# The query fold moved from the end of the tile loop to tile 5, with the raw weights as moving side

## The chip, the cores and the metric

The kernel runs on one core of a Trainium2 chip. A core has five engines, each with a queue of its own that it works through in order: TensorE (PE, matmuls; its weight loads are listed as PEld), VectorE (DVE), ScalarE (ACT), GpSimd (POOL) and SyncE (SP, which issues most of the DMA transfers). In this kernel PE reads SBUF and writes into eight PSUM banks of 128 x 512 floats, out of which ACT and DVE read. The metric is the device time of one launch in microseconds (us). Profiles come from one execution of the program under the hardware profiler.

## The reference

For 2048 tokens x of width 512 the reference computes two branches and mixes them with a gate per token.

```python
# branch A: linear attention, 32 heads of width 16
q, k, v = split(x @ wqkv)                       # [head, token, 16]
pq, pk  = q @ w_phi[head], k @ w_phi[head]      # a 16x16 matrix per head
phi(p)  = concat(softmax(p), softmax(-p))       # 32 features
kv = phi(pk)^T @ v ;  z = phi(pk)^T @ 1
a  = concat_heads(phi(pq) @ kv / (phi(pq) @ z + 1e-6)) @ wo
# branch B: product-key experts, 32 heads, top 1 of 16 x 16
s1, s2 = (x @ w_q)[..., :128] @ k1^T, (x @ w_q)[..., 128:] @ k2^T
e = 16 * argmax(s1) + argmax(s2)                # one of 256 experts per head
b = sum_heads gelu(x . u[e]) * v[e]             # the softmax over one candidate is 1
g = sigmoid(sum(x * gate_w)) ;  y = g * a + (1 - g) * b
```

Since w_phi acts on q right behind the projection, the kernel multiplies it into the weights: x @ (wq_A @ w_phi) gives pq in one product. This product of weights is called a fold; there is one for k and one for q. In the same way the keys k1 and k2 are multiplied into w_q, which gives score weights of 512 x 1024.

## The kernel before, in words

Tokens go in 16 tiles of 128 (NT = 16). Every matrix that feeds a large matmul is held as two parts, a rounded high part and the rest (xh and xl for the tokens, wah and wal, wbh and wbl, sh and sl, eh and el, uh and ul), and a product takes three matmuls per block of 128 (`proj` and `mm3`, lines 53 to 58 and 87). `split` (line 49) makes the two parts: ACT copies the high part, DVE subtracts.

The program has a fixed order per engine: the text of the kernel is the order of each queue. It has three stages.

Start (lines 251 to 295). PE does 16 matmuls on a zeroed tile, warm. v's weights come in (wbh, wbl), the first v tiles are projected, and k's weights are folded (`fold_k`): for each of 4 x 4 blocks the small matrix wp stands as 32 x 32 weights and 512 columns of the raw matrix move through, so that the output is the transposed fold. Four blocks of it are then turned on PE (`fold_turn`) and split into wah and wal.

Tile loop (line 304). Tile t loads x for tile t + 3, projects v (`vproj`) and k (`kproj`, whose four DVE operations take the softmax differences out of PSUM), takes exponentials on ACT (line 346), sums and reciprocals on DVE and a product on POOL (`ksoft`, lines 198 to 202), and every second tile sums phi(k)^T v into one bank (`kvacc`). Between these, the plan of line 302 spreads 16 steps that make the score weights: `score_w` multiplies a raw matrix wq with the keys into a bank of the tag tr, after every second one `score_planes` copies the bank as two planes of 16-bit halves into wpl (ACT), and SP turns the planes with one DMA transpose into wtp. One tile later `score_join` puts the halves together again (ACT, line 237), and splits them into sh (ACT, line 241) and sl (POOL, line 242). The raw matrices wq0 to wq15 share two buffers of 8 KB a partition, so each load waits for the matmuls on the matrix two before it. rawq, q's raw weights, is the last in this row.

PSUM has four banks of the tag mm and three of the tag tr, each handed out in turn.

In tile 15, while the last score block is joined, PE works through `fold_q` (line 140) in two halves, with the first scores of the query stage (`front_s`, line 246) behind each. fold_q holds the raw weights as PE's weights and moves 32 columns of wp, 128 times; the output is not transposed, and ACT and DVE split it straight from PSUM into wah and wal, which k no longer needs (lines 153 and 154). Then come tile 15's exponential and `ksoft`.

Query stage (from line 672). PE finishes the sums of phi(k) (`kvz`, lines 213 to 218, which needs the d of tiles 14 and 15 from POOL's line 202), projects the first q tile (`front_q`) and the first expert products (`front_p`), spreads z over all partitions (`z_final`) and goes into a loop of 15 turns with scores, masks, q, attention and output. For the first mask (`mid_mask`, line 537) `best` finds the maxima on DVE and SP turns the mask with a DMA transpose (et, line 482).

```python
    nc = bacc.Bacc("TRN2", target_bir_lowering=False, num_devices=1)
```

This line of the host part (892) sets up the program; the area of SBUF for descriptors that POOL would write has its default size of 16 KB a partition.

Of the kernel before, what the change touches and what calls it, by code (L numbers as in the profile page):

```python
# [9 lines left out]
F32 = mybir.dt.float32  # L10
F32R = mybir.dt.float32r
BF16 = mybir.dt.bfloat16
U16 = mybir.dt.uint16
# [3 lines left out]
ALU = mybir.AluOpType  # L17
# [3 lines left out]
P = 128  # L21
S = 2048
D = 512
NT = S // P
NK = D // P
# [10 lines left out]
def mix_kernel(ctx, tc, xT, wqT, wkT, wv, wphi, wo, wq, kk, ug, ev, cst, out):  # L36
    nc = tc.nc
    pe, dve, act, pool, sp = nc.tensor, nc.vector, nc.scalar, nc.gpsimd, nc.sync
# [4 lines left out]
    def mm_bank(name):  # L43
        return psum.tile([P, 512], F32, tag="mm", bufs=4, name=name)

    def tr_bank(name):
        return psum.tile([P, 512], F32, tag="tr", bufs=3, name=name)

    def split(hi, lo, src):
        act.copy(hi, src)  # L50
        dve.tensor_tensor(lo, src, hi, op=ALU.subtract)  # L51
# [8 lines left out]
    kvb = per.tile([P, 8, 32], F32, name="kvb")  # L60
# [10 lines left out]
    wah = per.tile([P, NK, D], F32R, name="wah")  # L71
    wal = per.tile([P, NK, D], F32R, name="wal")
# [38 lines left out]
    w1 = cb.enter_context(tc_pool("w1", "right"))  # L111
    wa_ = ca.enter_context(tc_pool("wl", "left"))
    home = lambda t: late if t % 4 > 1 else w1

    wp = w1.tile([P, NK, 32], F32, bufs=1, name="wp")
    warm = w1.tile([P, 384], BF16, bufs=1, name="warm")
    rawx = {}

    def stage(src, name, shape=None):
        t_ = wa_.tile(shape or [P, NK, D], F32, tag="st", bufs=2, name=name)  # L120
        if src is not None:
            sp.dma_start(t_, src)
        return t_

    def x_load(t):
        r = rawx[t] = wa_.tile([P, NK, P], F32, tag="xr", bufs=3, name=f"xr{t}")
        if t > 0:
            sp.dma_start(r, xT[t])
# [3 lines left out]
        (dve.tensor_copy if t < 3 else act.copy)(xh[:, t, ks], r[:, ks])  # L132
        dve.tensor_tensor(xl[:, t, ks], r[:, ks], xh[:, t, ks], op=ALU.subtract)

    fv = lambda a, q: a.rearrange("p k (b c) -> p (k b) c", c=P)[:, :, 32 * q:32 * q + 32]

    def four(name):
        return [tr_bank(f"{name}{q}") if q < 3 else mm_bank(f"{name}{q}") for q in range(4)]

    def fold_q(raw, wh, wl):  # L140
        o = four("foldq")
        for i in range(2):
            for k in (2 * i, 2 * i + 1):
                for b in range(NK):
                    for q in range(4):
                        r = slice(32 * q, 32 * q + 32)
                        c0 = (k * NK + b) * 32
                        pe.matmul(o[q][:, c0:c0 + 32], raw[r, b, k * P:(k + 1) * P], wp[r, b, :],
                                  start=True, stop=True, skip_group_check=True)
            yield  # L150
        for q in range(4):
            part = o[q].rearrange("p (g c) -> p g c", c=32)
            act.copy(fv(wh, q), part)
            dve.tensor_tensor(fv(wl, q), part, fv(wh, q), op=ALU.subtract)
        yield

    def fold_k(raw, tmp):
        o = four("foldk")
        for j in range(NK):
            for q in range(4):  # L160
                r = slice(32 * q, 32 * q + 32)
                pe.matmul(o[q][32 * j:32 * j + 32, :], wp[r, j, :], raw[r, j, :], start=True, stop=True,
                          skip_group_check=True)
        for q in range(4):
            (act.copy if q < 2 else dve.tensor_copy)(tmp[q], o[q])

# [53 lines left out]
    def score_w(i, raw):  # L220
        j, par = i // 2, i % 2
        if par == 0:
            wsP[j] = tr_bank(f"ws{j}")
        for c in range(4):
            pe.matmul(wsP[j][32 * c:32 * c + 32, :], kp[:, j // 4, par, :], raw[:, c, :],  # L225
                      start=(par == 0), stop=(par == 1))

    def score_planes(j):
        pl = wa_.tile([P, 2, D], U16, tag="wpl", bufs=1, name=f"wpl{j}")
        act.copy(pl, wsP.pop(j).bitcast(U16).rearrange("p (c j) -> p j c", j=2))  # L230
        tp = wa_.tile([P, 8, P], U16, tag="wtp", bufs=1, name=f"wtp{j}")
        sp.dma_start_transpose(tp, pl.rearrange("p j c -> p (j c)"))
        joins.append((j, tp))

    def score_join(j, tp):
        tj = wa_.tile([P, D], F32, tag="wtj", bufs=1, name=f"wtj{j}")
        act.copy(tj.bitcast(U16).rearrange("p (k n j) -> p j k n", j=2, n=P),
                 tp.rearrange("p (j k) n -> p j k n", j=2))
        js = slice(P * j, P * j + P)
        t3 = tj.rearrange("p (k e) -> p k e", k=NK)  # L240
        act.copy(sh[:, :, js], t3)
        pool.tensor_tensor(sl[:, :, js], t3, sh[:, :, js], op=ALU.subtract)
# [8 lines left out]
    pool.memset(warm, 0.0)  # L251
    tab = w1.tile([P, 1], F32, bufs=1, name="tab")
    pool.memset(tab, 0.0)
    x_load(0)
# [12 lines left out]
    x_load(2)  # L267
    wps = mm_bank("warm")
    for _ in range(16):
        pe.matmul(wps[:, :384], warm[:, 1:P + 1], warm, start=True, stop=True)  # L270
    for a in sa + sb:
        pool.memset(a, 0)
    pool.memset(kvb, 0.0)
    pool.memset(ones, 1.0)
    for k in (0, 2, 1, 3):
        if k == 0:
# [13 lines left out]
    v2 = vproj(2)  # L290
    fold_turn(tk, wah, wal)
    v2()
    raws = [stage(wq[0], "wq0")]
    raws.append(stage(wq[1], "wq1"))
    pool.tensor_copy(wm, cs[:, 128:160].rearrange("p (a b) -> p a b", b=F))

    def spare(src, name, shape):
        t_ = wa_.tile(shape, F32, tag="xr", bufs=3, name=name)
        sp.dma_start(t_, src)
        return t_  # L300

    plan = {0: 2, 2: 1, 3: 1, 4: 2, 6: 2, 8: 2, 10: 2, 12: 2, 13: 1, 14: 1}
    done = 0
    for t in range(NT):
        if t + 3 < NT:
            x_load(t + 3)
        if 2 < t < NT - 2:
            vproj(t)()
        kproj(t)
        old = [] if t == NT - 3 else list(joins)  # L310
        if old:
            joins.clear()
        for _ in range(plan.get(t, 0)):
            score_w(done, raws[done])
            done += 1
            if done + 1 < 16:
                raws.append(stage(wq[done + 1], f"wq{done + 1}"))
            elif done == 15:
                rawq = stage(wqT, "rawq")
            if done % 2 == 0:  # L320
                score_planes(done // 2 - 1)
        if t == 11:
            rawu = [spare(ug[:, 0:2], "rawu0", [P, 2, NU])]
        if t == 12:
            rawu.append(spare(ug[:, 2:4], "rawu1", [P, 2, NU]))
        if t == 13:
            rawe = [spare(ev[:, 0], "rawe0", [P, D])]
        if t % 2 == 0:
            for u in (t - 3, t - 2):
                if u >= 0:  # L330
                    kvacc(u)
        if 0 < t < NT - 2:
            x_split(t + 2)
        if t == NT - 2:
            score_join(*old.pop())
# [10 lines left out]
        act.activation(phis[t], phis[t], AF.Exp)  # L346
        if t == NT - 2:
            score_join(*joins.pop())
# [5 lines left out]
        for j, tp in old:  # L354
            score_join(j, tp)
    ca.close()
    w2 = ctx.enter_context(tc_pool("w2", "left"))
    zb = w2.tile([P, 1024], F32, name="zb", bufs=1)
# [339 lines left out]
    for a in range(NT - 1):  # L698
        n, b, z = a + 1, a - 1, a - 2
# [77 lines left out]
    a, b, z = NT - 1, NT - 2, NT - 3  # L777
# [50 lines left out]
    ch, cl, o = st8[b]["c"]  # L828
# [71 lines left out]
```

## Time and profile before

| what | value |
|---|---|
| time, median of 3 runs | 380.48 us (379.95 to 380.8) |
| span of the profiled execution, first to last instruction | 378.1 us |
| what lies around the span, against the median | 2.4 us (that execution's own run time is not listed apart) |
| granted clock of PE, mean | 1.000 |
| busy PE / DVE / ACT / POOL | 372.5 / 315.9 / 235.5 / 154.9 us |
| rawq: issue, landing | 108.9 us, 5.7 us later |
| transfers of wq (1 MB), median to landing | 6.0 us |
| transposes of wpl, median to landing | 7.3 us |

How to read the lines of a profile: a row of the timeline is start, duration, engine, line of the kernel, operation, output<-inputs, shapes (output<-input; for PE the shape of the weights stands in front) and count, and in brackets how long the engine had been idle before and what ended it. SPq is the DMA-issuing queue of SP. A row of the groups gives the busy time and the mean duration in ns behind the first bar, and the idle time before behind the second. fp32r is the rounded high-part type. DMA rows give the size in KB and the time from issue to landing.

### The profile page before, as it was taken

The page shows a single profiled execution, that of the slowest core. Times are in us where ns is not written, and L with a number is a line of the kernel's source. Part 1 is how long each engine was busy: PE and PEld are TensorE (multiplying, and loading weights), DVE is VectorE, ACT ScalarE, POOL GpSimd, SP SyncE. Part 2 cuts the span into 40 slices and gives each one's busy share as a digit, 9 for nine tenths or more (in the row PEclk, how much of TensorE's full clock was granted, in tenths as well). Part 3 has the DMA queues.
Part 4 walks back from the last instruction along what each step waited for, and adds up shares of the span by engine and source line. Part 5 has one row for each costly group of instructions (what it writes and reads, how often), then busy time and mean ns, then how long its engine had stood idle before and what let it go on. Part 6 is the DMA issues. An engine that isn't in the chain of part 4 may idle for free.

```text
span 378.1 us, 9073 instructions
## 1 busy us (share of the span) xinstructions
PE 372.5 (99%) x3613; PEld 294.3 (78%) x3613; DVE 315.9 (84%) x776; ACT 235.5 (62%) x420; POOL 154.9 (41%) x164
## 2 busy tenths in 40 slices
PE   8999999999999999999999999999999999999996
PEld 4766777777768888888878888888888888888775
DVE  4479866866868968879999999999999999999993
ACT  4436554644646345769668777696686686687741
POOL 1014435325325232946427335344454454364700
PEclk9999999999999999999999999999999999999999
DMA  7757878478592034242351452441532524523201
GB/s 272 307 187 259 258 218 237 157 222 237 188 305 84 3 85 83 73 83 76 80 99 49 105 84 57 85 100 32 121 62 65 127 56 72 126 52 77 64 34 57
DMA packets 72219, 46.69 MB, mean 123 GB/s; under 512 B 63600, under 2 KB 64496, under 8 KB 69872
## 3 DMA queue, kind: packets, MB, share of 16 engines
q1 hardware_dynamic: 71312, 45.24, 44.6%
q10 hardware_dynamic: 864, 0.87, 0.8%
q8 instruction: 28, 0.46, 0.5%
q14 instruction: 15, 0.12, 0.1%
HBM read 26.43 MB, written 4.19 MB: 81 GB/s over the span
## 4 chain that ended last, share of the span: by engine, by line
PE 97%; DMA 1%; ACT 0%; SPq 0%; DVE 0%; issue 0%; ACTq 0%; DVEq 0%
PE po L627 11%; PE s L56 8%; PE s L57 8%; PE s L58 8%; PE po L634 5%; PE pq L56 5%; PE pv L56 4%; PE pk L56 4%; PE ws L225 4%; PE pv L57 4%; PE pq L58 4%; PE pk L57 4%; PE pq L57 4%; PE pk L58 4%; PE pv L58 4%; PE oT L518 3%
## 5 line engine op out<-in xcount | busy, mean ns | idle before, releaser
L432 POOL TENSOR_TENSOR w<-d,zb 128x512 f32<-128x512 f32 x32 | 40.9, 1294 | 83.4 <-ACT d L426 81.1
L202 POOL TENSOR_TENSOR d<-d,st 128x1024 f32<-128x1024 f32 x16 | 31.0, 1935 | 74.4 <-DVE st L201 40.5
L56 PE MATMUL s<-sh,xh 128*128 128x512 f32 x128 | 51.0, 399 | 0.0
L57 PE MATMUL s<-sl,xh 128*128 128x512 f32 x128 | 49.9, 390 | 0.0
L58 PE MATMUL s<-sh,xl 128*128 128x512 f32 x128 | 49.8, 389 | 0.0
L426 ACT ACTIVATE d<-d 128x512 f32<-128x512 f32 x32 | 20.1, 632 | 38.0 <-DVE d L98 29.3
L467 POOL TENSOR_TENSOR d<-d,st 128x512 f32<-128x512 f32 x30 | 31.2, 1062 | 28.5 <-DVE st L461 25.6
L509 ACT COPY pt<-tp 128x1024 uint16<-128x1024 uint16 x28 | 36.4, 1369 | 1.0 <-PE kvacc L209 1.0
L346 ACT ACTIVATE d<-d 128x1024 f32<-128x1024 f32 x16 | 17.0, 1064 | 28.5 <-DVE d L100 28.5
L499 ACT COPY pl<-d 128x1024 uint16<-128x1024 uint16 x28 | 29.2, 1045 | 4.4 <-POOL d L467 4.4
L58 PEld LDWEIGHTS s<-sh,xl 128*128 128x128 f32 x128 | 24.0, 188 | 5.1
L56 PEld LDWEIGHTS s<-sh,xh 128*128 128x128 f32 x128 | 24.0, 188 | 4.7
L57 PEld LDWEIGHTS s<-sl,xh 128*128 128x128 f32 x128 | 24.1, 188 | 4.5
L56 PE MATMUL pq<-wah,xh 128*128 128x512 f32 x64 | 26.7, 418 | 0.0
L56 PE MATMUL pv<-wbh,xh 128*128 128x512 f32 x64 | 26.0, 407 | 0.0
L436 DVE TENSOR_REDUCE st<-d 128x32 f32<-128x512 f32 x32 | 21.7, 683 | 5.0 <-ACT d L426 3.5
L57 PE MATMUL pv<-wbl,xh 128*128 128x512 f32 x64 | 25.2, 394 | 0.3 <-DVE wbl L51 0.3
L200 DVE TENSOR_REDUCE st<-d 128x64 f32<-128x1024 f32 x16 | 19.5, 1218 | 7.0 <-ACT d L346 7.0
L56 PE MATMUL pk<-wah,xh 128*128 128x512 f32 x64 | 25.3, 396 | 0.0
L58 PE MATMUL pv<-wbh,xl 128*128 128x512 f32 x64 | 25.1, 392 | 0.0
L58 PE MATMUL pq<-wah,xl 128*128 128x512 f32 x64 | 25.1, 392 | 0.0
L57 PE MATMUL pk<-wal,xh 128*128 128x512 f32 x64 | 25.0, 391 | 0.0
(177 smaller groups left out, 1029.5 us busy)
## 6 DMA issues: line engine op xcount, KB each, us to landing
wq<-wq SPq DMA_DIRECT2D x16, 1024.0 KB, 6.0
xr<-xT SPq DMA_DIRECT2D x15, 256.0 KB, 6.0
y<-ot SPq DMA_DIRECT2D x15, 256.0 KB, 2.3
rawk<-wkT SPq DMA_DIRECT2D x1, 1024.0 KB, 6.1
rawq<-wqT SPq DMA_DIRECT2D x1, 1024.0 KB, 5.7
rawo<-wo SPq DMA_DIRECT2D x4, 256.0 KB, 3.8
rawu<-ug SPq DMA_DIRECT2D x2, 258.0 KB, 6.3
rawv<-wv ACTq DMA_DIRECT2D x2, 256.0 KB, 4.2
```

The costliest lines, as they stand in the source:

```text
L56: pe.matmul(o, ah, bh, start=(first and i == 0), stop=False)
L57: pe.matmul(o, ah, bl, start=False, stop=False)
L58: pe.matmul(o, al, bh, start=False, stop=(last and i == n - 1))
L200: dve.tensor_reduce(st[:, 64:128], g64(d), axis=AX.X, op=ALU.add)
L202: pool.tensor_tensor(g64(d), g64(d), b64(st[:, 128:192]), op=ALU.mult)
L426: act.activation(hs(d, i), hs(d, i), AF.Exp)
L432: pool.tensor_tensor(hs(e["w"], i), hs(e["ph"], i), hs(zb, i), op=ALU.mult)
L436: dve.tensor_reduce(pair(e["st"][:, 64:128])[:, :, i], hs(e["ph"], i), axis=AX.X, op=ALU.add)
L467: eng.tensor_tensor(g64(d)[:, gs_], g64(d)[:, gs_], r[:, gs_].unsqueeze(2).to_broadcast([P, 32, F]), op=ALU.mult)
L499: act.copy(pl, e["ph"][:, halves[i]].bitcast(U16).rearrange("p (c j) -> p j c", j=2))
L509: act.copy(p16[:, :, 4 * i:4 * i + 4, :], e["tp"][i].rearrange("p (j g) n -> p j g n", j=2))
L627: pe.matmul(po, a, b, start=(i == 0), stop=False)
```

## The change

- The q fold moves from tile 15 to tile 5 and takes the form of the k fold: wp as 32 x 32 weights, the raw weights as moving side. Both folds now call one function, `fold`.
- Its output is transposed and must be turned. This is done as for the score weights: a copy into two planes of 16-bit halves (ACT), a DMA transpose (SP), a join (ACT) into a new tile wqf. Two of the four blocks go out in tile 5, two in tile 7; each is joined at the end of the tile behind it. `score_planes` becomes `turn_planes`, which also takes the function for the join.
- In tile 15 wqf is split into wah and wal with four ordinary splits, ahead of the score matmuls.
- rawq is loaded in the place of wq6, and each later wq load goes out one step later, wq7 behind the fold.
- wpl has two buffers instead of one, wtp three instead of one; wqf is new (8 KB a partition). The tile warm is gone, its matmuls read kvb, which is zeroed first for that.
- The descriptor area of POOL has 2 KB instead of 16.

```diff
-    warm = w1.tile([P, 384], BF16, bufs=1, name="warm")
+    warm = kvb.rearrange("p g c -> p (g c)").bitcast(BF16)
...
-    def fold_q(raw, wh, wl):
-        o = four("foldq")
-        for i in range(2):
-            for k in (2 * i, 2 * i + 1):
-                for b in range(NK):
-                    for q in range(4):
-                        r = slice(32 * q, 32 * q + 32)
-                        c0 = (k * NK + b) * 32
-                        pe.matmul(o[q][:, c0:c0 + 32], raw[r, b, k * P:(k + 1) * P], wp[r, b, :],
-                                  start=True, stop=True, skip_group_check=True)
-            yield
-        for q in range(4):
-            part = o[q].rearrange("p (g c) -> p g c", c=32)
-            act.copy(fv(wh, q), part)
-            dve.tensor_tensor(fv(wl, q), part, fv(wh, q), op=ALU.subtract)
-        yield
-
-    def fold_k(raw, tmp):
-        o = four("foldk")
+    def fold(raw, name):
+        o = four(name)
         for j in range(NK):
             for q in range(4):
                 r = slice(32 * q, 32 * q + 32)
                 pe.matmul(o[q][32 * j:32 * j + 32, :], wp[r, j, :], raw[r, j, :], start=True, stop=True,
                           skip_group_check=True)
+        return o
+
+    def fold_k(raw, tmp):
+        o = fold(raw, "foldk")
...
-    def score_planes(j):
-        pl = wa_.tile([P, 2, D], U16, tag="wpl", bufs=1, name=f"wpl{j}")
-        act.copy(pl, wsP.pop(j).bitcast(U16).rearrange("p (c j) -> p j c", j=2))
-        tp = wa_.tile([P, 8, P], U16, tag="wtp", bufs=1, name=f"wtp{j}")
+    def turn_planes(j, o, then):
+        pl = wa_.tile([P, 2, D], U16, tag="wpl", name=f"wpl{j}")
+        act.copy(pl, o.bitcast(U16).rearrange("p (c j) -> p j c", j=2))
+        tp = wa_.tile([P, 8, P], U16, tag="wtp", bufs=3, name=f"wtp{j}")
         sp.dma_start_transpose(tp, pl.rearrange("p j c -> p (j c)"))
-        joins.append((j, tp))
+        joins.append((then, j, tp))
+
+    def q_join(q, tp):
+        view = wqf.rearrange("p k d -> p (k d)").bitcast(U16).rearrange("p (g c j) -> p j g c", j=2, c=P)
+        act.copy(view[:, :, :, 32 * (q % 4):32 * (q % 4) + 32],
+                 tp.rearrange("p (j k) (b c) -> p j (k b) c", j=2, c=32))
...
-    pool.memset(warm, 0.0)
+    pool.memset(kvb, 0.0)
...
+    wqf = wa_.tile([P, NK, D], F32, name="wqf", bufs=1)
...
-            if done + 1 < 16:
-                raws.append(stage(wq[done + 1], f"wq{done + 1}"))
-            elif done == 15:
+            if done + 1 == 6:
                 rawq = stage(wqT, "rawq")
+            elif done + 1 < 16:
+                load_wq()
             if done % 2 == 0:
-                score_planes(done // 2 - 1)
+                turn_planes(done // 2 - 1, wsP.pop(done // 2 - 1), score_join)
+        if t == 5:
+            fq = fold(rawq, "foldq")
+            load_wq()
+        if t in (5, 7):
+            for q in ((3, 0) if t == 5 else (1, 2)):
+                turn_planes(20 + q, fq[q], q_join)
...
-            fq = fold_q(rawq, wah, wal)
-            next(fq)
+            for k in range(NK):
+                split(wah[:, k, :], wal[:, k, :], wqf[:, k, :])
             front_s(0, 0)
-            next(fq)
             front_s(0, 1)
             kvacc(NT - 3)
-            next(fq)
...
-    nc = bacc.Bacc("TRN2", target_bir_lowering=False, num_devices=1)
+    nc = bacc.Bacc("TRN2", target_bir_lowering=False, num_devices=1,
+                   dynamic_dma_scratch_size=2048)
```

More of the change, by code (lines that the diff above doesn't have):

```diff
@@ L269, in mix_kernel @@
     for _ in range(16):
-        pe.matmul(wps[:, :384], warm[:, 1:P + 1], warm, start=True, stop=True)
+        pe.matmul(wps[:, :384], warm[:, 1:P + 1], warm[:, :384], start=True, stop=True)
     for a in sa + sb:
         pool.memset(a, 0)
-    pool.memset(kvb, 0.0)
     pool.memset(ones, 1.0)
@@ L292, in mix_kernel, with load_wq @@
     v2()
-    raws = [stage(wq[0], "wq0")]
-    raws.append(stage(wq[1], "wq1"))
+    raws = []
+    def load_wq():
+        raws.append(stage(wq[len(raws)], f"wq{len(raws)}"))
+    load_wq()
+    load_wq()
+    wqf = wa_.tile([P, NK, D], F32, name="wqf", bufs=1)
     pool.tensor_copy(wm, cs[:, 128:160].rearrange("p (a b) -> p a b", b=F))
@@ L315, in mix_kernel @@
             done += 1
[L316 to L318 removed]
+            if done + 1 == 6:
                 rawq = stage(wqT, "rawq")
+            elif done + 1 < 16:
+                load_wq()
             if done % 2 == 0:
[L321 removed]
+                turn_planes(done // 2 - 1, wsP.pop(done // 2 - 1), score_join)
+        if t == 5:
+            fq = fold(rawq, "foldq")
+            load_wq()
+        if t in (5, 7):
+            for q in ((3, 0) if t == 5 else (1, 2)):
+                turn_planes(20 + q, fq[q], q_join)
         if t == 11:
@@ L334, in mix_kernel @@
         if t == NT - 2:
-            score_join(*old.pop())
+            then, j, tp = old.pop()
+            then(j, tp)
         elif t == NT - 1:
@@ L338, in mix_kernel @@
                 split(eh[:, k, :], el[:, k, :], rawe[k])
-            fq = fold_q(rawq, wah, wal)
-            next(fq)
+            for k in range(NK):
+                split(wah[:, k, :], wal[:, k, :], wqf[:, k, :])
             front_s(0, 0)
-            next(fq)
             front_s(0, 1)
             kvacc(NT - 3)
-            next(fq)
         act.activation(phis[t], phis[t], AF.Exp)
         if t == NT - 2:
-            score_join(*joins.pop())
+            then, j, tp = joins.pop()
+            then(j, tp)
         if t == 13:
@@ L353, in mix_kernel @@
         ksoft(t)
-        for j, tp in old:
-            score_join(j, tp)
+        for then, j, tp in old:
+            then(j, tp)
     ca.close()
```

1 line of the change is left out of this document (removed).

## The prediction

> **What bounds the kernel now.** I read the page from the top: busy times, slices, queues, the chain that ended last.
>
> ```profile
> span 378.1 us, 9073 instructions
> PE 372.5 (99%) x3613; PEld 294.3 (78%) x3613; DVE 315.9 (84%) x776; ACT 235.5 (62%) x420; POOL 154.9 (41%) x164
> ...
> PEclk9999999999999999999999999999999999999999
> ...
> q1 hardware_dynamic: 71312, 45.24, 44.6%
> q10 hardware_dynamic: 864, 0.87, 0.8%
> ...
> PE 97%; DMA 1%; ACT 0%; SPq 0%; DVE 0%; issue 0%; ACTq 0%; DVEq 0%
> ```
>
> TensorE (PE) is busy 372.5 of 378.1 us and makes up 97% of the chain, at full granted clock. So a microsecond of PE work is worth a microsecond, as long as nothing else stands just behind PE. That last condition has to be read stage by stage. The stage of the change is the end of the tile loop, so I asked for the busy time of each engine there (columns: stretch, length, then PE, PEld, DVE, ACT, POOL busy with counts, clock, DMA share, GB/s):
>
> ```profile
> 118.50:134.00 15.50, 15.22 (x323) 12.84 (x320) 15.33 (x23) 6.92 (x15) 5.12 (x3) 1.00 0.10 20
> ```
>
> In these 15.5 us VectorE (DVE) is busy 15.33. PE and DVE are both full: whoever takes work off PE here meets DVE.
>
> **The PE work that goes and comes.** From the timeline of PE, the matmuls on both sides of the two halves of the old q fold (116.48 to 119.06, 121.34 to 123.92), and of the k fold, whose form (32x32 weights, raw weights as 512 moving columns) the new q fold shares:
>
> ```profile
> 12.19 0.39 PE L58 MATMUL pv<-wbh,xl 128*128 128x512 f32 x1
> 12.50 1.14 PE L162 MATMUL foldk<-rawk,wp 32*32 32x512 f32 x32
> ...
> 13.91 0.40 PE L57 MATMUL pv<-wbl,xh 128*128 128x512 f32 x1
> ...
> 116.48 0.39 PE L58 MATMUL pk<-wah,xl 128*128 128x512 f32 x1
> ...
> 118.72 0.50 PE L56 MATMUL s<-sh,xh 128*128 128x512 f32 x1
> 119.06 0.40 PE L57 MATMUL s<-sl,xh 128*128 128x512 f32 x1
> ...
> 121.34 0.39 PE L58 MATMUL s<-sh,xl 128*128 128x512 f32 x1
> ...
> 123.92 0.40 PE L57 MATMUL s<-sl,xh 128*128 128x512 f32 x1
> ```
>
> From 119.06 to 121.34 lie ten matmuls, 0.228 us each from start to start. Without a fold between them, the two outer matmuls of each pair would be two steps, 0.46 us, apart. So each half of the old fold costs 2.58 - 0.46 = 2.12 us, together 4.24 us. The k fold costs 13.91 - 12.19 - 0.46 = 1.26 us, and I take that for the q fold at tile 5, where PE is as full. PE alone would gain 4.24 - 1.26 = 2.98 us.
>
> **Tile 5: is the raw matrix there in time?** The load of rawq takes the place of wq6 in the SP queue, wq6 that of wq7, and wq7 is issued behind the fold. Rows of SP's queue, of the transfers issued at 43 to 46 us (size, us to landing), of PE and of ScalarE (ACT):
>
> ```profile
> 43.72 1.19 SPq L122 DMA_DIRECT2D wq<-wq  x2
> ...
> wq<-wq SPq DMA_DIRECT2D x1, 1024.0 KB, 4.9
> ...
> wq<-wq SPq DMA_DIRECT2D x1, 1024.0 KB, 7.8
> ...
> 50.97 0.39 PE L58 MATMUL pk<-wah,xl 128*128 128x512 f32 x1
> ...
> 56.73 1.93 PE L225 MATMUL ws<-wq,kp 128*32 128x512 f32 x16
> ...
> 53.98 1.06 ACT L346 ACTIVATE d<-d 128x1024 f32<-128x1024 f32 x1 [3.96 <-DVE d L100]
> ```
>
> rawq, issued at 43.72, lands at about 48.6; the fold starts behind the last pk at about 51.3: no wait, with 2.7 us to spare. wq7 goes out when the fold ends, about 52.4. It lands at 57.3 if it has the engines to itself (4.9) and at 60.2 if it queues behind another megabyte (7.8). PE wants it for the second half of the score pair, at 56.73 + 1.26 + 0.96 = 58.9. So this wait lies between 0 and 1.3 us. In front of wq7 stand only one transpose and one quarter-megabyte x load, so the row of 4.9 is the nearer and I take 0.
>
> Behind wq7 on SP stand the four new transposes and the next x loads; nobody needs those before the end of tile 6 or 8. Before, the transpose of each score block waited for the one wtp buffer; three buffers take that wait away, but only ACT's joins come behind it.
>
> **ACT's new work.** From the groups of instructions (count, busy us, mean ns):
>
> ```profile
> L237 ACT COPY wtj<-wtp 128x1024 uint16<-128x1024 uint16 x8 | 10.8, 1346 | 0.7 <-DMA wtp<-wpl 0.7
> ...
> L230 ACT COPY wpl<-ws 128x1024 uint16<-128x1024 uint16 x8 | 8.1, 1012 | 12.8 <-PE ws L225 12.6 <-ACT uh L50 0.2
> ```
>
> Four copies into halves (4 x 1.01) and four joins (4 x 1.35) are 9.4 us more on ACT, spread over tiles 5 to 8. Two copies, 2.0 us, fall in front of the tile's x split and exponential, into the 3.96 us in which ACT waits for DVE (row 53.98): hidden. In tile 7 the second copy also waits for a buffer that an earlier transpose still reads. If that cover were gone, DVE would start the next tile's sums up to 2 us late, but it idles 2.5 us before each odd tile (row 107.95 below is such a gap). I take 0 for PE. The splits of wah and wal in tile 15 replace four copies and four subtracts of the same count.
>
> **What is late next.** The rows that gate PE behind the removed fold, in order of time:
>
> ```profile
> 107.95 0.69 DVE L94 TENSOR_REDUCE st<-pk 128x32 f32<-128x512 f32 x1 [2.55 <-PE pk L58]
> ...
> 118.39 1.36 ACT L237 COPY wtj<-wtp 128x1024 uint16<-128x1024 uint16 x1
> ...
> 120.48 1.29 POOL L242 TENSOR_TENSOR sl<-wtj,sh 128x512 fp32r<-128x512 f32 x1 [2.12 <-ACT sh L241]
> ...
> 122.53 2.28 DVE L51 TENSOR_TENSOR el<-rawe,eh 128x512 fp32r<-128x512 f32 x2
> ...
> 123.67 2.06 ACT L153 CAST wah<-foldq 128x512 fp32r<-128x512 f32 x4 [2.22 <-PE foldq L148]
> ...
> 124.73 2.47 DVE L154 TENSOR_TENSOR wal<-foldq,wah 128x512 fp32r<-128x512 f32 x4
> ...
> 129.09 1.94 POOL L202 TENSOR_TENSOR d<-d,st 128x1024 f32<-128x1024 f32 x1 [5.43 <-DVE st L201]
> ...
> 131.59 1.34 SPq L482 DMA_TRANSPOSE et<-eq  x1
> ...
> et<-eq SPq DMA_TRANSPOSE x1, 2.9
> ...
> 132.16 0.71 PE L217 MATMUL kvacc<-ones,d 128*32 128x1 f32 x64
> ...
> 134.93 0.36 PEld L537 LDWEIGHTS <-et 128*128 128x128 bf16 x8
> ```
>
> From 107.95 on DVE, ACT and POOL run one series that starts with the end of pk13 on PE and never waits for the fold: ACT's wah copies do (2.22 us), but DVE reaches wal only at 124.73, behind el. In the clock of before (everything behind tile 5 shifts by 1.26) it opens three gates:
> - Gate 1: ACT joins the last score block at 118.39, and its part of sl is ready at 120.48 + 1.29 = 121.77. The second matmul of the second score half needs it; without the fold PE is there at 123.92 - 4.24 = 119.68. PE waits 2.09 and restarts with one step of 0.34 (as from 118.72 to 119.06) instead of 0.23. Of the 4.24, 2.04 are left.
> - Gate 2: tile 15's d is ready at 129.09 + 1.94 = 131.03; PE comes for it (kvz, L217) at 132.16 - 2.04 = 130.12. It waits 0.91; 1.13 are left.
> - Gate 3: et lands at 131.59 + 2.9 = 134.49; PE comes to load it at 134.93 - 1.13 = 133.80. It waits 0.69; 0.44 are left.
>
> Behind gate 3 PE ran without a wait before, and still does, since no other engine is later than PE by then. The sum: 1.26 paid at tile 5, 0.44 got back, +0.82 us.
>
> The subtracts of wal now read wqf from SBUF instead of PSUM:
>
> ```profile
> L51 DVE TENSOR_TENSOR wbl<-rawv,wbh 128x512 fp32r<-128x512 f32 x4 | 2.7, 689 | 0.1
> ...
> L154 DVE TENSOR_TENSOR wal<-foldq,wah 128x512 fp32r<-128x512 f32 x4 | 2.5, 676 | 0.0
> ...
> L132 DVE CAST xh<-xr 128x512 fp32r<-128x512 f32 x2 | 0.8, 423 | 1.4 <-DMA xr<-xT 1.4
> ```
>
> They lie on the series of gates 2 and 3. Bounds: 1.14 each if POOL runs beside them (el, 2.28 for two), 0.42 each as the fastest row of that size on DVE (L132). The nearest row has the same operation and homes, L51 with 689 against 676 ns: 0.05 us later for four. With that the sum is +0.87; I say +0.9, span 379.0.
>
> [...]
>
> **Ring and warm-up.** Both queues in use are hardware queues; no transfer is issued by POOL, so the ring's size costs nothing either way. What it frees, 14 KB, is what wqf (8), two wtp (4) and one wpl (2) need. At the start kvb's memset takes the place of warm's:
>
> ```profile
> 0.73 0.42 POOL L251 MEMSET warm<- 128x384 bf16 x1 [0.29 <-POOLq L892]
> ...
> 1.21 5.15 PE L270 MATMUL warm<-warm 128*128 128x384 bf16 x16 [1.21 <-POOL tab L253]
> ...
> 1.58 0.32 POOL L273 MEMSET kvb<- 128x256 f32 x1
> ```
>
> 0.1 us at most either way, and the first real matmuls wait for loads: 0.
>
> **Rivals.**
> 1. The earlier transposes pull the series up. With three wtp buffers the score blocks are turned and joined sooner, POOL is done sooner and no longer runs beside el (1.14 us each, against 0.69 for L51), and sl, d and et come earlier; if all three gates open before PE gets there, PE's whole 2.98 us remains: 377.5. For it: 97% PE on the chain. Against it: el alone gives 0.9 us, and the rest of the DVE series hangs on pk13, not on a join. It decides (over 0.2% faster) only from 1.6 us of et's 134.49 on.
> 2. The DVE series is shorter than I sum it (the wal subtracts by up to 4 x 0.25 = 1.0 at L132's pace): gates 2 and 3 open earlier by as much, +0.9 falls towards -0.1; 380.4 to 381.2. Already 0.15 us less makes it no measurable change.
> 3. wq7 lands late: up to 1.3 us more at tile 6, which all later gates inherit: 381.8 to 382.7.
> 4. The 2.1 us pause at gate 1 costs PE its clock. The warm-up matmuls step at (5.15 - 0.51)/15 = 0.31 us for 384 columns, or 0.41 for 512, against 0.228 later. Five microseconds at that pace lose 2.2: 383.6. Against it: the pause has PE work on both sides.
>
> [...]
>
> **How the numbers follow.** The median is 380.48, 2.4 us above the profiled span; I add the sum to it: 381.4. 0.2% (0.76 us) is about what a measurement of this kernel can tell from no change. Chances: my forecast 0.52 (its own range 381.0 to 381.8, a fifth of it within 0.2%), rival 1 0.10, rival 2 0.20, rival 3 0.14, rival 4 0.04. Faster 0.10, same 0.10 + 0.20 = 0.30, slower 0.42 + 0.14 + 0.04 = 0.60. The range 380.2 to 382.6 leaves out rivals 1 and 4 and the end of 3.
>
> **What would show it.** Right: 32 fold matmuls in about 1.1 us near 51.3 with no PE wait before them; PE idle of about 2 us in the second score half with sl as its releaser, then waits on d (POOL) and on et. Wrong: PE without waits in tile 15; a PE wait on wq in tile 6; a granted clock under 1.00.

## The result, and the profile after

The changed kernel takes 382.79 us in the median of 6 runs (381.41 to 383.06), the kernel before 380.51 in 6 runs of the same chip: a ratio of 1.0049, 95% interval 1.0033 to 1.0065. By the ratio that is 1.9 us slower, and the two medians lie 2.3 us apart; 0.9 was forecast. The profiled execution, at 381.41 us, was the fastest of the six. Its page (busy times; the chain) and, in the last line, the window of the last tile:

```profile
span 379.4 us, 8887 instructions
...
PE 370.7 (98%) x3517; PEld 290.7 (77%) x3517; DVE 317.1 (84%) x776; ACT 243.5 (64%) x428; POOL 154.0 (41%) x163
...
PE 90%; DVE 5%; DMA 2%; ACT 1%; issue 1%; POOL 1%; ACTq 0%; POOLq 0%; DVEq 0%
...
118.50:134.00 15.50, 12.64 (x243) 9.94 (x242) 14.23 (x21) 7.65 (x14) 6.51 (x5) 1.00 0.03 8
```

PE has 1.8 us less to do (372.5 before) and the span is 1.3 us longer. In the window PE is busy 12.64 of 15.5 us where it was busy 15.22, and the chain runs through DVE, DMA, ACT and POOL for 9% where all but 3% was PE. The work that went has left holes. PE's timeline shows what filled them (start, duration, instruction, idle before and its releaser):

```profile
51.31 0.39 PE L58 MATMUL pk<-wah,xl 128*128 128x512 f32 x1
51.63 1.14 PE L143 MATMUL foldq<-rawq,wp 32*32 32x512 f32 x32
...
58.37 1.92 PE L210 MATMUL ws<-wq,kp 128*32 128x512 f32 x16
...
122.00 0.49 PE L56 MATMUL s<-sh,xh 128*128 128x512 f32 x1 [0.89 <-ACT sh L231]
123.35 0.50 PE L57 MATMUL s<-sl,xh 128*128 128x512 f32 x1 [0.86 <-POOL sl L232]
...
132.63 0.71 PE L202 MATMUL kvacc<-ones,d 128*32 128x1 f32 x64 [0.84 <-POOL d L187]
...
136.37 0.36 PE L538 MATMUL mk<-wm,et 128*128 128x16 bf16 x8 [0.70 <-DMA et<-eq]
```

The new fold runs without a wait. Then come three waits: for the halves of the last score block, for d of tile 15, and for et's transpose. The releasers are the forecast's gates 1, 2 and 3, in that order. What releases them (POOL, DVE, and SP's issue of et with its landing):

```profile
109.48 0.69 DVE L94 TENSOR_REDUCE st<-pk 128x32 f32<-128x512 f32 x1 [2.50 <-PE pk L58]
...
122.02 1.27 POOL L232 TENSOR_TENSOR sl<-wtj,sh 128x512 fp32r<-128x512 f32 x1 [2.11 <-ACT sh L231]
...
126.27 2.49 DVE L51 TENSOR_TENSOR wal<-wqf,wah 128x512 fp32r<-128x512 f32 x4
...
133.14 1.94 SPq L483 DMA_TRANSPOSE et<-eq  x1
...
et<-eq SPq DMA_TRANSPOSE x1, 3.2
```

The series starts 1.53 us later than before (109.48 against 107.95), sl is ready 1.52 us later (123.29 against 121.77) and et is issued 1.55 us later (133.14 against 131.59). It kept its length and moved as a block, and PE now stands behind it.

### The profile page after: what moved, and what is told of

Its sections match the earlier page's. It is cut to its first block, busy times and chain, and to the rows that moved or that the text cites. A ratio compares the mean times of both kernels' runs of the same rounds, so it can differ in the third digit from the quotient of the medians.

```text
span 379.4 us, 8887 instructions
## 1 busy us (share of the span) xinstructions
PE 370.7 (98%) x3517; PEld 290.7 (77%) x3517; DVE 317.1 (84%) x776; ACT 243.5 (64%) x428; POOL 154.0 (41%) x163
## 4 chain that ended last, share of the span: by engine, by line
PE 90%; DVE 5%; DMA 2%; ACT 1%; issue 1%; POOL 1%; ACTq 0%; POOLq 0%; DVEq 0%
PE po L628 11%; PE s L56 8%; PE s L57 7%; PE s L58 7%; PE po L635 5%; PE pq L56 4%; PE pv L56 4%; PE pv L57 4%; PE pv L58 4%; PE pq L58 4%; PE pq L57 4%; PE ws L210 3%; PE pk L56 3%; PE pk L57 3%; PE pk L58 3%; PE oT L519 3%
## 5 line engine op out<-in xcount | busy, mean ns | idle before, releaser
L57 PE MATMUL pq<-wal,xh 128*128 128x512 f32 x64 | 25.0, 390 | 0.0
```

What stands on the lines that cost most here:

```text
L57: pe.matmul(o, ah, bl, start=False, stop=False)
```

## The experiments

Each was compared with the kernel before on the same chip. The last column counts runs whose mean granted clock is 0.996 or less: a stretch of 3.41 us at half clock, as three of the profiles below show one, takes 0.5 x 3.41 / 380 = 0.0045 from the mean. The kernel before had medians of 380.93 us beside the rows without a q fold, with the 2 KB ring, with idle matmuls and of the change again, 380.48 beside the last two rows, and 380.55 beside the others; so the ratios are to be compared, not the medians.

| Kernel | median us (runs) | ratio to before, 95% | runs with clock <= 0.996 |
|---|---|---|---|
| change again, unaltered | 382.68 (6) | 1.0054 [1.0037, 1.0072] | 4 of 6; with the first six runs 7 of 12 |
| before without a q fold | 382.07 (10) | 1.0025 [1.0005, 1.0044] | 7 of 10 |
| before with the 2 KB ring | 381.67 (10) | 1.0008 [0.9995, 1.0022] | 0 of 10 |
| change, pause filled with idle matmuls | 382.39 (7) | 1.0050 [1.0029, 1.0070] | 2 of 7 |
| change, mask matmul later | 381.58 (12) | 1.0028 [1.0005, 1.0051] | 6 of 12 |
| before, mask matmul later | 380.17 (12) | 0.9989 [0.9978, 1.0000] | 0 of 12 |
| change, pause filled with v of tile 14 | 381.92 (10) | 1.0029 [1.0014, 1.0044] | 0 of 10 |
| both of these | 380.37 (12) | 0.9999 [0.9982, 1.0015] | 1 of 12 |
| change without el's subtract | 381.78 (12) | 1.0030 [1.0019, 1.0041] | 6 of 12 |
| both, and two orders on ACT | 380.28 (12) | 1.0006 [0.9989, 1.0023] | 1 of 12 |

Of the kernel before, none of the runs beside these was at 0.996 or less.

**The change once more.** The theory is the three gates; the rival is that a loss of clock does part of it.

> The changed kernel once more, unaltered. Gates theory (the fold's cost at tile 5 is paid, the saving at tile 15 is lost to three waits, for sl, for d and for et): the profile shows a PE wait before the second score half, before kvz of tile 15 and before the first mask, about 0.9 + 0.9, 0.8 and 0.7 us, and the span is about 1 us over the one of before. Clock theory (the pause of about 2 us for sl costs PE its clock in those executions where it falls whole into one of the chip's activity windows): the timed runs fall into two groups, mean granted clock about 1.00 and about 0.994, and the second group is 1 to 2 us longer. Without the clock theory all runs have one clock and lie near 381.4.

Its profile caught what the first did not. Windows of busy time (stretch, length, PE, PEld, DVE, ACT, POOL busy with counts, clock, DMA share, GB/s) and PE's timeline:

```profile
118.00:123.41 5.41, 3.66 (x15) 2.45 (x14) 4.25 (x8) 4.06 (x6) 3.31 (x3) 1.00 0.11 24
123.41:126.82 3.41, 3.07 (x7) 2.48 (x8) 3.41 (x5) 3.02 (x5) 2.18 (x2) 0.50 0.00 0
126.82:137.90 11.08, 9.43 (x238) 8.00 (x236) 9.00 (x15) 3.24 (x11) 2.67 (x2) 1.00 0.37 40
```

```profile
122.40 0.50 PE L56 MATMUL s<-sh,xh 128*128 128x512 f32 x1 [1.24 <-ACT sh L231]
123.75 0.80 PE L57 MATMUL s<-sl,xh 128*128 128x512 f32 x1 [0.85 <-POOL sl L232]
124.34 0.63 PE L58 MATMUL s<-sh,xl 128*128 128x512 f32 x1
124.77 0.63 PE L56 MATMUL s<-sh,xh 128*128 128x512 f32 x1
...
133.48 0.71 PE L202 MATMUL kvacc<-ones,d 128*32 128x1 f32 x64
...
137.89 0.36 PE L538 MATMUL mk<-wm,et 128*128 128x16 bf16 x8 [1.37 <-DMA et<-eq]
```

Two waits of 1.24 and 0.85 us with one matmul between them, and for 3.41 us the granted clock is 0.50: the matmuls step 0.43 us instead of 0.23. That costs half of 3.41, 1.7 us of PE. Part is absorbed, since PE would have waited for d next and now does not (row 133.48). Over the 12 runs of the change, the five above 0.996 have a mean of 382.24 us and the seven others 383.08: 0.84 us per run that loses its clock, and 0.5 us in the mean of all. Even those that keep it are 0.8 us above the forecast of 381.4.

**Before, with the q fold left out.** q is then projected with its raw weights, so the fold is missing from the result; all else of before stays. This removes the 4.24 us at tile 15 and adds nothing at tile 5.

```diff
-            fq = fold_q(rawq, wah, wal)
-            next(fq)
+            for k in range(NK):
+                split(wah[:, k, :], wal[:, k, :], rawq[:, k, :])
             front_s(0, 0)
-            next(fq)
...
-            next(fq)
```

> The kernel before without any q fold (q's raw weights are split instead, so the fold is left out of the computation), nothing put in at tile 5. Gates theory: of the 4.24 us of PE work that go, the three waits take back all but about 0.4: 380.1, ratio 0.999; the profile shows the same three waits. Clock theory on top: up to 1.7 us more in part of the runs, median up to 381.5. Face value of PE's chain (no gates): 376.3, ratio 0.989.

It came out slower than before, by 0.25% (0.05% to 0.44%). The gates alone had a gain of 0.1%, and a loss of up to 1.0 us was forecast only with the clock on top; but the profiled execution, at 382.14 us, kept its clock. PE's timeline has the reason for it:

```profile
121.54 0.50 PE L56 MATMUL s<-sh,xh 128*128 128x512 f32 x1 [0.88 <-ACT sh L241]
122.89 0.50 PE L57 MATMUL s<-sl,xh 128*128 128x512 f32 x1 [0.85 <-POOL sl L242]
132.17 0.71 PE L217 MATMUL kvacc<-ones,d 128*32 128x1 f32 x64 [0.87 <-POOL d L202]
133.16 2.05 PE L661 MATMUL z<-cs,zc 128*128 128x128 f32 x16 [0.28 <-ACT zc L681]
137.29 0.36 PE L535 MATMUL mk<-wm,et 128*128 128x16 bf16 x8 [2.07 <-DMA et<-eq]
```

0.88 + 0.85 + 0.87 + 2.07 = 4.67 us of waits took the place of 4.24 us of matmuls. et landed 4.6 us after its issue here, and the gates had been summed with 2.9. So the fold's place in tile 15 was worth nothing to begin with: not in this execution, and not in the ten runs together. Seven of the ten lost their clock, which the kernel before never shows. So losing it does not need the new fold. In the times of this kernel the loss cannot be seen apart (379.87 to 383.29 us with it, 381.86 to 382.14 without).

**Before, with the 2 KB ring alone.**

```diff
-    nc = bacc.Bacc("TRN2", target_bir_lowering=False, num_devices=1)
+    nc = bacc.Bacc("TRN2", target_bir_lowering=False, num_devices=1,
+                   dynamic_dma_scratch_size=2048)
```

> The kernel before with only the descriptor area of POOL at 2 KB. If the ring and the addresses that move with it have no part: 380.5, ratio 1.000, first v matmuls as before (the second wbh copy at 5.8 us). If they delay the first loads (the profile of the changed kernel has that copy at 6.4 us and everything behind it 0.38 us later): 380.9, ratio 1.001.

1.0008, an interval that holds 1. Its profile was useful for something else, the landing of et (DMA issues; then PE):

```profile
et<-eq SPq DMA_TRANSPOSE x1, 4.8
```

```profile
136.99 0.36 PE L537 MATMUL mk<-wm,et 128*128 128x16 bf16 x8 [1.17 <-DMA et<-eq]
```

Before took 2.9 us for the same transpose, and PE did not wait. The landing differs from execution to execution: 2.9 in before and 3.0 with its mask matmul later, 4.8 and 4.6 in two others (the ring, and no fold), 3.2 and 4.3 in the two of the change. Gate 3 therefore closes even in the kernel before in some executions (the profile with the 2 KB ring is one).

**Is gate 3 the one that decides?** From the start of the first mask matmul to the end, the profiles give 378.1 - 135.04 = 243.06 us for before, 243.11 with the ring, 243.01 without the fold, and 243.03 and 243.01 for the change. So everything behind it is of one length, and a span is that start plus 243. The row of before:

```profile
135.04 0.35 PE L537 MATMUL mk<-wm,et 128*128 128x16 bf16 x8
```

Moving this matmul behind the first score half of the next block opens the gate, in the change and, as a control, in before:

```diff
-        if not left:
+        if not left and a:
             mid_mask(a)
         front_s(n, 0)
+        if not a:
+            mid_mask(a)
```

> The changed kernel with the matmuls of the first mask put behind the first score half of the next tile (s1 of tile 1), so that PE has 2.7 us of work while et lands. Third-gate theory: in every profile so far the span ends 243.0 to 243.2 us after the first mask matmul, whatever came before it, so the landing of et decides; with the mask out of the way the span ends 0.7 to 2.2 us earlier than the changed kernel's (379.4 and 380.9): about 378.7, median 381.0, ratio 1.000 to 1.002. A clock drop can still cost up to 0.9. If the landing of et does not decide, nothing changes: 382.7.

> The kernel before with the same exchange of mask and score half. Third-gate theory: before waits for et too wherever it lands later than 3.4 us after its issue (4.8 us and a PE wait of 1.17 us in the profile with the smaller ring), so its median falls by 0.5 to 1.0 to about 380.0, ratio 0.998, and its spread shrinks. If before has no such wait: ratio 1.000.

In the change, gate 3's wait is gone (the last row), but the waits at gates 1 and 2 stay:

```profile
122.20 0.49 PE L56 MATMUL s<-sh,xh 128*128 128x512 f32 x1 [1.29 <-ACT sh L231]
123.55 0.50 PE L57 MATMUL s<-sl,xh 128*128 128x512 f32 x1 [0.86 <-POOL sl L232]
132.84 0.71 PE L202 MATMUL kvacc<-ones,d 128*32 128x1 f32 x64 [0.89 <-POOL d L187]
...
138.46 0.36 PE L538 MATMUL mk<-wm,et 128*128 128x16 bf16 x8
```

The span of this execution is the 378.7 us that was expected. The ratio, 1.0028, is nearer to 1 than the 1.0049 and 1.0054 of the change but above the 1.000 to 1.002 that was expected, and the intervals overlap. The twelve times fall into two groups: of the six with the clock above 0.996 five lie at 380.14 to 380.54 us and one at 382.61, median 380.43; the six others at 380.89 to 383.98, median 382.5. The groups lie 2.1 us apart. That is more than the half-clock stretch explains: it costs 1.7, of which gate 2's wait of 0.89 should absorb a part. No profile caught such an execution, so the rest stays open. A changed kernel that keeps its clock and does not wait for et is about as fast as before (380.43 against 380.55). In before the same exchange brings 0.11% (0 to 0.22%), half of what was expected, but the late runs are gone: its twelve lie at 379.98 to 380.83 us, while of the 35 runs of before beside them 13 lie at 381.02 to 382.09. So gate 3 does cost the kernel before time in some of its runs.

**What takes the clock away?** Two fillings of gate 1's pause. The first puts twelve matmuls that compute nothing between the two score halves:

```diff
             front_s(0, 0)
+            wf = tr_bank("fill")
+            for _ in range(12):
+                pe.matmul(wf[:, :384], warm[:, 1:P + 1], warm[:, :384], start=True, stop=True)
             front_s(0, 1)
```

> The changed kernel with 12 matmuls of 384 bf16 columns on zeros, into an unused bank, between the two score halves of tile 15, so that PE works through most of the pause for sl. Gates theory: the waits for d and et stay (0.8 and 0.7 us), nothing gained on the undisturbed executions, span 379.0 to 379.4. Clock theory: no run has a clock under 0.998, so the median falls to about 381.4, 1.0 to 1.5 us under that of the changed kernel in the same job. If the clock has no part in it, the median stays at that of the changed kernel, about 382.8.

```profile
120.93 2.12 PE L346 MATMUL fill<-kvb 128*128 128x384 bf16 x12
132.60 0.71 PE L202 MATMUL kvacc<-ones,d 128*32 128x1 f32 x64 [0.85 <-POOL d L187]
133.60 3.68 PE L667 MATMUL z<-cs,zc 128*128 128x128 f32 x16 [0.28 <-ACT zc L687]
```

```profile
133.75:137.16 3.41, 3.41 (x16) 3.23 (x16) 1.75 (x4) 1.66 (x5) 0.72 (x1) 0.50 0.92 83
```

PE no longer waits at gate 1, but neither forecast of the clock theory came true: two of seven runs lost their clock (7 of 12 without the filling; too few to call it rarer), and the median is 382.39, not 381.4. In the profiled execution the loss came at another place, behind gate 2: z, at a clock of 0.50, took 3.68 us where it takes 2.05. The time did not move (1.005). So the first pause is one place where the clock can go, not the only one. The second filling moves real work there, the v projection of tile 14, which turn 1 then no longer has to do:

```diff
             front_s(0, 0)
+            v14 = vproj(NT - 2)
             front_s(0, 1)
...
-            v14, v15 = vproj(NT - 2), vproj(NT - 1)
+            v15 = vproj(NT - 1)
```

> The changed kernel with v's projection of tile 14 (12 matmuls, 2.7 us of work that stood in the query stage) moved into the pause for sl, between the two score halves. Gates theory: the pause is filled with work that is needed anyway and is then missing later, so the 2.7 us come back except for what the waits for d and et still take; as et still gates (landing about 136.3 to 138), the first mask does not start earlier, but the 2.7 us of v work are gone behind it: span 376.7 to 378.2, median 380.0, ratio 0.998. Clock theory: no drop behind the first pause; clock 0.999 to 1.000 in all runs but those that drop at the waits for d and et. If PE were not what bounds the query stage, the gain would be lost there: 382.7.

> Both exchanges in the changed kernel: v's projection of tile 14 in the pause for sl, and the first mask behind the score half. Gates theory: of the three waits only that for d is left (about 0.5 us), so the fold's smaller cost comes through: the changed kernel less 2.7 and less 0.7 to 2.2: span about 375.7 to 376.5, median 378.3, ratio 0.993 to the kernel before. Clock theory: every run at 0.998 or more, small spread. If the gain stops earlier, another engine (DVE in the query stage) has become the bound.

```profile
123.62 0.39 PE L56 MATMUL s<-sh,xh 128*128 128x512 f32 x1
...
132.60 0.71 PE L202 MATMUL kvacc<-ones,d 128*32 128x1 f32 x64 [0.50 <-POOL d L187]
...
136.83 0.36 PE L541 MATMUL mk<-wm,et 128*128 128x16 bf16 x8 [1.19 <-DMA et<-eq]
```

These are rows of the kernel with v of tile 14 alone. With the pause at gate 1 gone, none of ten runs lost its clock; what is left is 0.50 for d and 1.19 for et. So the clock held, as its theory had it, but the 2.7 us did not come back: 1.0029 where 0.998 was expected. The span still ends 243.0 us after the first mask matmul (379.8 - 136.83 = 242.97), although turn 1 has 2.7 us less to do. All of it is gone within turn 1: from that mask matmul to the first q product of turn 1 it is 161.83 - 136.83 = 25.00 us, in the change 161.40 - 136.37 = 25.03. In between PE now waits 1.32 and 0.84 us for ACT; the other 0.5 us goes at the two groups of matmuls behind these waits. With the mask moved as well the time is that of before (0.9999, where 0.993 was expected). The profile of that kernel also shows the forecast's rival 3 in the flesh, once in the eight profiles of kernels that hold the new fold:

```profile
60.27 1.06 PE L210 MATMUL ws<-wq,kp 128*32 128x512 f32 x8 [0.62 <-DMA wq<-wq]
```

wq7 landed 7.0 us after its issue there, against 5.7 to 6.2 in the seven others.

**Two ACT orders in turn 1.** In the kernel with both, PE waits 1.31 and 0.85 us for ACT in turn 1, the same two waits:

```profile
154.47 0.74 PE L194 MATMUL kvacc<-v,d 128*32 128x16 f32 x64 [1.31 <-ACT v L174]
...
160.46 1.21 PE L522 MATMUL oT<-pt,kvb 64*32 64x128 f32 x32 [0.85 <-ACT kvb L661]
```

The edit puts behind those two what ACT did ahead of them:

```diff
-        soft_exp(a)
         if a == 1:
             v15()
+        soft_exp(a)
...
             coef(b)
+            if a == 1:
+                kv_final()
             c_planes(b)
         if a == 1:
-            kv_final()
```

> v14gap_mask with two ScalarE orders changed in turn 1 (the copy of v of tile 15 goes ahead of the soft part of tile 1, and the last kv step goes ahead of the planes of c), so that the matmuls of turn 1 no longer wait 1.32 and 0.84 us for ScalarE. If those two waits were lost time: span some 1.5 to 2.2 us under that of v14gap_mask (379.5), so about 377.5, median 378.4 to 379, 0.994 to 0.996 of the kernel before, TensorE's clock at 0.998 or more in nearly all runs. If they were covered by a later wait (VectorE's work of the query stage): median 380.2 to 380.6, ratio 0.999 to 1.0005.

```profile
162.04 0.50 PE L631 MATMUL po<-wbh,xh 128*128 128x512 f32 x1 [1.29 <-ACT xh L526]
```

The two waits went and this one of 1.29 us came behind them, on the same engine. The profiled span fell from 379.5 to 377.8, but 1.35 of this was there before tile 15 (DVE's series starts at 109.19 against 110.54: start-up, and the late wq7 of the other profile). The median stayed (380.28, 1.0006), about as expected if the two waits were covered by a later one, though by one for ACT and not for DVE. No version tried is faster than before beyond the measurement.

**The change without el's subtract.** The low part of the expert values is zero, so that part is not computed; 2.29 us leave DVE's series ahead of gates 2 and 3:

```diff
+    pool.memset(el.bitcast(F32), 0.0)
...
-                split(eh[:, k, :], el[:, k, :], rawe[k])
+                act.copy(eh[:, k, :], rawe[k])
```

> The kernel after with el's subtract left out (the low part of the expert values is zeroed once at the start, so that part of the computation is left out); everything else is as it was. Theory A (gates 2 and 3 are set by VectorE's series in front of them): the 2.29 us of el's two subtracts go from that series, d of tile 15 and the issue of et's transpose come up to 2.3 us earlier, the waits of 0.84 and 0.70 in front of kvacc and the mask matmul shrink by about their whole size, gate 1 keeps its 0.9 + 0.86, the first mask matmul starts 1 to 1.5 us earlier than in the profiles of after (136.4 to 137.9); median about 381, with TensorE's clock still dropping in some of the runs, as gate 1 is left. Theory B (those gates are set by something else, the DMA's landing alone or ScalarE): first mask matmul at 136.4 or later, median 382.2 to 382.8 as before this edit.

```profile
122.25 0.49 PE L56 MATMUL s<-sh,xh 128*128 128x512 f32 x1 [0.87 <-ACT sh L231]
123.60 0.50 PE L57 MATMUL s<-sl,xh 128*128 128x512 f32 x1 [0.86 <-POOL sl L232]
...
133.41 0.71 PE L202 MATMUL kvacc<-ones,d 128*32 128x1 f32 x64
...
136.30 0.35 PE L539 MATMUL mk<-wm,et 128*128 128x16 bf16 x8
```

```profile
124.31 3.48 DVE L51 TENSOR_TENSOR wal<-wqf,wah 128x512 fp32r<-128x512 f32 x4
```

The waits at gates 2 and 3 are gone and gate 1's stayed, as the theory of the gates has it. But this execution lost its clock behind gate 1 (windows of the pause and of the 3.41 us behind it, granted clock the third number from the end):

```profile
121.41:124.82 3.41, 1.72 (x6) 1.23 (x7) 3.38 (x7) 3.38 (x8) 2.55 (x2) 1.00 0.00 0
124.82:128.23 3.41, 3.41 (x55) 2.33 (x58) 3.41 (x5) 1.45 (x2) 0.62 (x1) 0.50 0.00 0
```

A loss of clock by itself makes PE late for gate 2, as in the second profile of the change, so the missing waits prove little. What shows the gates' cause is that d is ready 21.89 us after the start of DVE's series (109.74), in the change 23.10, and et is issued 22.44 us after it, in the change 23.66. Both come 1.2 us earlier, more than the 0.84 and 0.70 us that PE waited there. The series got shorter by 1.2 to 1.3 us only, not 2.29, because wal now takes 3.48 us in place of 2.49: its first subtract takes 1.68 us and the three others 0.68. In the change it is el's first subtract that takes 1.69 us, and its second 0.68. Both times POOL is still at work on d of tile 14, and the long subtract ends 0.55 us behind it. So 1.0 us of the series is no work of el's but falls to the subtract that comes first; that POOL is its cause was not tested.

With half the clock behind gate 1, the mask matmul started at 136.30 all the same. The median of 381.78 lies between the two theories, 0.8 us above the first. The six runs that kept their clock (median 381.7) are no faster than the six that did not (381.8); why, these runs do not show.

## Why the prediction was right, and where it was short

- **The sum, against the profiled execution.** Forecast 379.0 for the span, measured 379.4: the three gates were right, and the size for this execution. Of the shift of 1.53 us at the start of DVE's series, 0.38 was there at the k fold already (12.88 against 12.50). This is start-up: over the twelve profiles the k fold starts anywhere from 12.50 to 13.55, whether changed or not. With that the forecast would have been 379.4. A little of this agreement is luck: et landed 0.3 us later after its issue than summed, and was issued 0.14 us earlier.
- **The fold at tile 5**, 1.26 by the k fold. From the k fold to DVE's series it is 109.48 - 12.88 = 96.60 us against 107.95 - 12.50 = 95.45: 1.15. In the other profiles of the change, with PE unhindered, it is 1.15 to 1.35. Right.
- **rawq in time, no wait: right.** wq7 at 0 of 0 to 1.3 us: right for PE in the first profile, but narrowly. It landed 6.2 us after its issue, not 4.9, and its weight load waited 0.66 us while PE still had matmuls (weight loads and DMA issues of the change):

```profile
59.18 0.20 PEld L210 LDWEIGHTS ws<-wq,kp 128*32 128x32 f32 x8 [0.66 <-DMA wq<-wq]
```

```profile
wq<-wq SPq DMA_DIRECT2D x1, 1024.0 KB, 6.2
```

  One profile in eight has PE itself waiting.
- **The gates.** Gate 1: 2.09 forecast, 0.89 + 0.86 = 1.75 measured, with a matmul between them and so two restarts; the first of the two is for sh from ACT, which the forecast did not list. Gate 2: 0.91 forecast, 0.84 measured. Gate 3: 0.69 and 0.70. Right, and in the forecast order.
- **wal from SBUF: right.** 2.49 us for four against 2.47 from PSUM. So SBUF as the source made them no shorter here.
- **The ring at 0: right** (1.0008, 0.9995 to 1.0022). ACT's copies and joins delayed no PE instruction: from 44 to 110 us PE is busy for all of the 66 us.
- **The median, short by 1.4 us** (1.0 by the ratio). The 382.79 lies 0.2 us above the range of 380.2 to 382.6; by the ratio, 1.0049 x 380.48 = 382.3, it is inside. Two terms were too small. The step "Rival 4, the pause costs PE its clock" got 0.04, with the argument that the pause has PE work on both sides, and a price of 2.2 us; by the mean clock it happened in 7 of 12 runs, and it costs 0.84 us there, 0.5 in the mean. And gate 3 was summed with one landing of et, 2.9 us, the shortest of the profiles; it takes up to 4.8. Before had 134.93 - 134.49 = 0.44 us in hand there and the change has none, so each late landing costs the change up to 0.4 us more. Together that is at most 0.9 us; against 1.4 the rest is not accounted for. A granted clock under 1.00 stood on the forecast's own list of signs of being wrong, and it came.

The length of the pause alone does not decide over the clock: in the second profile of the change 1.24 + 0.85 us were followed by a stretch at 0.50, with the mask matmul later 1.29 + 0.86 us were not. In three profiles (the second of the change, the filled kernel, the change without el's subtract) such a stretch lasts 3.41 us. In the clock records of the twelve profiles each stretch at full clock lasts a whole number of steps of 3.413 us (35, 38, 71, 74, 75, 109 or 110; 372.05 us are 109 steps in before and in the first profile of the change). Counted in such steps from a change of the clock, borders can be placed over the whole span; they stand at another place of it each time. In the first profile of the change the clock next falls at 378.15, at the end; 76 and 75 steps before that are borders at 118.74 and 122.15. They cut the pause in two, and PE is busy 2.52 and 2.56 of 3.41 us on the two sides. In the second profile all of the pause but its last 0.34 us lies between the borders at 119.99 and 123.41; PE is busy 1.66 us, and the clock falls at 123.41 (two rows of the first, one of the second):

```profile
118.74:122.15 3.41, 2.52 (x12) 1.79 (x10) 2.25 (x4) 3.21 (x4) 1.30 (x2) 1.00 0.03 5
122.15:125.57 3.42, 2.56 (x11) 1.84 (x12) 3.42 (x5) 3.42 (x7) 3.04 (x2) 1.00 0.00 0
```

```profile
120.00:123.41 3.41, 1.66 (x7) 0.80 (x5) 2.96 (x5) 3.38 (x6) 1.31 (x2) 1.00 0.00 0
```

The three other profiles with a pause at gate 1 fit: without el's subtract all but its first 0.03 us lies in one such window of 3.413 us, PE is busy 1.72 us of it, and the clock falls; with the mask matmul later and without a fold a border cuts it, PE is busy 2.02 us or more on each side, and the clock stays. So what fits these five is that the same pause costs the clock when nearly all of it falls into one window, and that differs from execution to execution. The busy share alone does not decide: the filled kernel lost its clock behind a window with 2.29 us busy (130.33 to 133.75), and the kernel with v of tile 14 alone kept it behind one with 2.23 (134.51 to 137.92). What else counts was not found.

## What to carry to other kernels

A chain that is 97% PE says that PE ends last, not that PE's work is worth its length: list the releasers of the next waits and how far behind PE they stand, and the value of a removed matmul ends there (here 4.24 us of matmuls were worth nothing). Price a gate that a DMA opens with the spread of its landing over several executions, not with the one profiled. Where work is taken out of a full PE, put other useful work into the hole: a pause of 2 us in two pieces may also cost the clock behind it (1.24 + 0.85 us did in one profile). Filling it with the v projection kept the clock in all ten runs here (idle matmuls did in five of seven), but the 2.7 us that the filling saved elsewhere went to the next waits, so look for those too.

## What the runs showed of the hardware that was not expected

- Waits of 1.24 and 0.85 us, 0.5 us of work between them, were followed by 3.41 us at a granted clock of 0.50 in one profile of the change; by the mean clock 7 of its 12 runs lost as much. Waits of 0.85 and 0.28 us were followed by the same in one profile of the filled kernel.
- In the clock records of the twelve profiles the clock changed only at borders a whole number of steps of 3.413 us apart, whose place in the span differs from execution to execution. The pause at gate 1 cost the clock in the two profiles in which nearly all of it lay within one such step (1.66 and 1.72 of 3.41 us busy) and in none of the three in which a border cut it near its middle.
- The transpose of et, the same transfer in every kernel, lands 2.9 to 4.8 us after its issue. What delays it was not found.
- The first subtract of el takes 1.67 to 1.73 us and the second 0.68, in all eleven profiles that have el; without it the first of wal takes 1.68. Each time POOL's d runs beside it.
